# Linear attention and experts in one kernel: attention's short sums in named banks, leading rows' products later, the expert part's gathers in one written order

## The chip, the cores and the metric

The kernel runs on one core of a Trainium2 chip. Its engines are TensorE (PE in the rows, its weight loads PEld), VectorE (DVE), ScalarE (ACT), GpSimd (POOL) and SyncE (SP). The metric is the device time of one execution in microseconds (us); the kernel before has a median of 881.65 over three runs (881.14 to 881.79). All data is float32; a product of two float32 numbers is made from high and low parts in three passes.

## The reference

```
proj = x @ w_phi; proj -= max|proj|          # per row, 128 features
phi  = [exp(proj), exp(-proj)]               # 256 features, for q and k
kv   = phi(k).T @ v;  z = sum phi(k)         # per batch and head
x    = (phi(q) @ kv) / (phi(q) @ z + 1e-6)   # 8 batches x 8 heads x 576 rows x 64
x    = x as [4608 rows, 512]
logits = x @ w_gate;  e = argmax(logits);  gate = softmax(logits)[e]
out[row] = gate * (relu(x[row] @ w1[e]) @ w2[e])      # 8 experts, 512 -> 1024 -> 512
```

Each row of x goes to one of 8 experts; which one is known only at run time.

## The kernel before, in words

**Attention (0 to about 388 us).** 16 units of work, each two heads of two batches, in two halves (A and B, one per batch). In a half TensorE projects q and k (`ps_proj`), transposes exponentials (`pt`), adds up keys times values over the half (`pk`, the long sum, 30 matmuls), copies it out (`kvT`, by ACT at L410), multiplies it once more with small constants (`pf`, L419, copied to `kf` by VectorE at L430) and forms the outputs of the unit before (`pn`, L448). The order on TensorE is written by hand: `half` (L511) walks 30 slots and `chain` (L259) ties each matmul behind the one before; `book` (L506) puts other steps at a slot's number. One half is about 11.7 us long, a slot about 0.39.

**The pool of sums.** `pk` and the short sums `pf`, `prk` (counts that give each row its rank within its expert), `pc` and `pl` share a PSUM pool `ps_kv` of two buffers that are handed out in turn. `count_ranks` (L729) is booked at `RANK_AT` for three of the four groups of batches, the reduce and the three selects (L745 to L756, which read `prk`) at the slots behind it.

**The leading rows.** After three of four groups, the expert with most rows so far is picked (`pick_lead`, `find`), a 0/1 matrix `b` is built by VectorE (L838), and 54 products of three columns, `pl` (`find_rows`, L846, L849 and L850), give the numbers of its first 3 x 128 rows; `fetch` gathers them (POOL, L861), so that the expert part can begin with them.

**Expert part (from about 388 us).** Rows are sorted by expert into blocks of 128. A pair of blocks runs through `pair_first` (four times 24 matmuls of 256 columns into `pm`, L1123 to L1125), a relu by ACT (`hh`, L1130) and a remainder by VectorE (`hl`, L1131), and `pair_second` (four times 12 matmuls of 512 columns into `po`, L1143 to L1145); 19 pairs, then single blocks. A pair lasts about 22.5 us. `write` scales `po` with the row's gate into `ob` (ACT, L1191) and scatters it to the output (POOL, L1193). Each pair needs gathers on POOL: the rows `xg` (whole rows for the first pairs, from the fifth in eight quarter gathers, transposed by VectorE at L1099 into `px`), and the gates `gate`. In the code the gathers of pair u+2 and the gates of pair u+1 are called in the first quarter of pair u; where they stand on POOL the scheduler of the framework decides.

Of the kernel before, what the change touches and what calls it, by code (L numbers as in the profile page):

```python
# [9 lines left out]
F32 = mybir.dt.float32  # L10
# [46 lines left out]
def tile_linear_attention_moe(  # L57
# [36 lines left out]
    sg = late.enter_context(tc.tile_pool(name="sg", bufs=1, side="right"))  # L94
    ps_kv = late.enter_context(tc.tile_pool(name="ps_kv", bufs=2, space=PSUM, side="right"))
    hold = mid.enter_context(tc.tile_pool(name="hold", bufs=1, side="right"))
# [5 lines left out]
    ps_tr = early.enter_context(tc.tile_pool(name="ps_tr", bufs=2, space=PSUM, side="left"))  # L102


    w_bd = const.tile([P, 2 * F], F32, name="w_bd")
# [15 lines left out]
    for _ in range(WARM):  # L121
        pw = ps_kv.tile([P, 4, P], F32, name="pw", tag="pk")
        T.matmul(pw, ones, ones.unsqueeze(1).to_broadcast([P, 4, P]), start=True, stop=True)
# [75 lines left out]

    TOP_AT, RANK_AT, LEAD_AT = 78, 106, 166  # L200

# [48 lines left out]
    def behind(m, other):  # L250

        tc.add_manual_dep(
            m.ins,
            other.ins.name,
            mybir.DependencyInfo(mybir.DependencyClass.NoSync, mybir.DependencyReason.DATA),
            reason="order of the engine",
        )

    def chain(m):  # L259
# [109 lines left out]
    def kv_steps(st, bb):  # L369


        def step(hh, i, c, j):
            vh, vl = st["v"]
            if (hh, i, j) == (0, 0, 0):
                st["pk", bb] = ps_kv.tile([P, 2, 2 * F], F32, name="pk", tag="pk")
            n = D if j == 1 else D + 1
            kh, kl, s0 = st["kp", c]
            return T.matmul(  # L378
                st["pk", bb][0:n, hh, :],
                (vl if j == 1 else vh)[:, 2 * (c + (bb if c == 8 else 0)) + hh, 0:n],  # L380
                (kl if j == 2 else kh)[:, s0 + hh].rearrange("p s f -> p (s f)"),
                start=(hh, i, j) == (0, 0, 0),
                stop=(hh, i, j) == (1, 4, 2),
            )

        def whole(hh, i, c):
            if (hh, i) == (0, 0):
                st["pk", bb] = ps_kv.tile([P, 2, 2 * F], F32, name="pk", tag="pk")
# [264 lines left out]
    def route(g, lgc, c0, n, final=None):  # L653
# [55 lines left out]
        def count():  # L709
            if final:  # L710
                pc = ps_kv.tile([P, E], F32, name="pc", tag="pk")
                T.matmul(pc, ones, r["base"], start=True, stop=False)
# [92 lines left out]
    def lead():  # L805
# [4 lines left out]
        def pick_lead():  # L810
            pc = ps_kv.tile([P, E], F32, name="pc", tag="pk")
            T.matmul(pc, ones, bases[-1], start=True, stop=True)
# [33 lines left out]
        def find_rows():  # L846
            pl = ps_kv.tile([P, NLEAD], F32, name="pl", tag="pk")
# [12 lines left out]
    def fetch_rows(out, source, index, rows):  # L860
        return G.indirect_dma_start(  # L861
            out=out,
# [4 lines left out]
            oob_is_err=False,  # L867
        )

    def gather_rows(index, rows, after=None):  # L870
# [6 lines left out]
    def gather_quarters(b):  # L877


        xg = xgp.tile([P, 4, P], F32, name="xg")  # L880
        quarters = x_dram.rearrange("t (q d) -> (t q) d", q=4)
        for c in range(4):
            behind(fetch_rows(xg[:, c, :], quarters, qidx[:, c, b : b + 1], 4 * NT), st["experts"])
        return xg

    def gather_gates(b, after):
        gate = xgp.tile([P, XW], F32, name="gate", bufs=6)
        index, rows = (gidx0, NEARLY * P) if b < NLEAD else (gidx, NT)
        behind(fetch_rows(gate, g_dram, index[:, b : b + 1], rows), after)
        return gate  # L890
# [14 lines left out]
    for u, st in enumerate(units):  # L905
# [9 lines left out]
        if u % NPR == 0 and u > 0:  # L915
# [8 lines left out]
    kv_copy(prev, 1)  # L924
    slot[0] += 100
    take(len(queue))
# [45 lines left out]
    def tokens_of():  # L972

        pp = ps_kv.tile([P, NB], F32, name="pp", tag="pk")
        for j in range(NTILE):
# [9 lines left out]
    def quarters_of():  # L985
# [6 lines left out]
        )  # L992
        pq = ps_kv.tile([P, 4, NB], F32, name="pq", tag="pk")
        for c in range(4):
# [74 lines left out]

    def gather(u):  # L1070
        if u >= lim[0]:
            return
        for b in blocks(u):
            if ("xg", b) not in st:
                if b < NLEAD:
                    st["xg", b] = early_rows[b]
                elif by_quarters(u):
                    st["xg", b] = gather_quarters(b)
                else:
                    st["xg", b] = gather_rows(gidx[:, b : b + 1], NT, st.get("experts"))  # L1080

    def gates(u):
        if u < lim[0]:
            for b in blocks(u):
                if ("gate", b) not in st:
                    st["gate", b] = gather_gates(b, st["experts"])

# [25 lines left out]
    def pair_first(u, j, half=None):  # L1113
# [20 lines left out]
    def pair_second(u, j, half=None):  # L1134
        if j == 0:
# [10 lines left out]
        if j == 3 and half != 0:  # L1146
            for b, po in zip(blocks(u), st["po", u]):
                write(b, po)

    def first_product(u, n):  # L1150
# [37 lines left out]
    def write(b, po):  # L1188
# [3 lines left out]
        index = sidx0[:, b : b + 1] if b < NLEAD else sidx[:, b : b + 1]  # L1192
        G.indirect_dma_start(  # L1193
            out=out,
# [4 lines left out]
            oob_is_err=False,  # L1199
        )  # L1200

    r1 = route(NG - 1, lgc, 0, 6, False)
# [49 lines left out]
    quarters_of()  # L1252
    gates(1)
    gather(2)
# [13 lines left out]
    AHEAD_W = (((1, 2), (0, 7)), ((1, 3), (1, 4)), ((2, 0), (1, 5)), ((2, 1), (1, 6)))  # L1268
    for u in range(1, NPAIR):
        for j in range(4):  # L1270
            pair_first(u, j)
            if j > 1:
                x_parts(u + 1, j - 2)
            if (u, j) != (1, 0):
                pair_second(u - (j == 0), (j - 1) % 4)
            if j == 0:
                gather(u + 2)
                gates(u + 1)
            for du, k in AHEAD_W[j]:
                weights(u + du, k)  # L1280

    first_product(NPAIR, 0)
    pair_second(NPAIR - 1, 3)
# [107 lines left out]
```

## Time and profile before

| | before |
|---|---|
| median of 3 runs | 881.65 us (881.14 to 881.79) |
| the profiled execution | 882.15 us, of which the span 880.5 |
| TensorE busy | 865.2 us, 98% of the span |
| VectorE, ACT, POOL busy | 71%, 65%, 64% |
| mean granted clock | 0.991 of full |

The profile is of one execution. A row of the timeline gives the start and the length of one instruction (or of a run of equal ones, xN), its engine, its line, output <- inputs and, in brackets, how long the engine stood idle before it and what released it. The granted clock of TensorE has two levels, 1.0 and 0.5 of full speed; a number between is a mean over a stretch.

### The profile page before, as it was taken

To read this page: it belongs to the slowest core of one execution; us is meant where nothing else is said; L and a number is where in the kernel's file an instruction comes from. 1 tells how busy PE (TensorE), PEld (TensorE's weight loads), DVE (VectorE), ACT (ScalarE), POOL (GpSimd) and SP (SyncE) were. 2 spreads that over 40 slices of the span, in tenths; PEclk is the share of its full clock that TensorE was granted. 3 is DMA by queue.
4 is the path that set the end of the run, shared out by engine and by line. 5 is a ranking of instruction groups with operands and counts; after the bars stand their busy time and mean duration, and the time that the engine had idled before them with its cause. 6 is when DMAs were issued, how large, how long until landed. Compare 5 with 4: busy or idle time off the path is not lost. (4 is left out here: it accounts for less than half of the span.)

```text
span 880.5 us, 18049 instructions
## 1 busy us (share of the span) xinstructions
PE 865.2 (98%) x6605; PEld 811.7 (92%) x6605; DVE 623.7 (71%) x1044; ACT 572.6 (65%) x874; POOL 560.1 (64%) x407
## 2 busy tenths in 40 slices
PE   9999999999999999999899999999999999999997
PEld 6999999999999999999699999999999999999985
DVE  7678778887887788649487666666666666666451
ACT  6888888888888888653375555555555555555562
POOL 5667667776676677643666888867666666643342
PEclk9999999999999999899999999999999999999999
DMA  6233334333343333351344144541444653435650
GB/s 204 85 102 97 106 112 97 78 97 107 112 113 112 112 104 79 88 195 29 85 153 116 54 165 133 157 136 49 143 138 137 200 181 113 153 116 176 209 185 18
DMA packets 69692, 106.65 MB, mean 121 GB/s; under 512 B 13726, under 2 KB 31646, under 8 KB 69600
## 3 DMA queue, kind: packets, MB, share of 16 engines
q1 hardware_dynamic: 59312, 84.50, 31.9%
q0 software_dynamic: 9616, 20.81, 7.7%
q8 instruction: 53, 0.87, 0.4%
q14 instruction: 39, 0.32, 0.1%
q10 hardware_dynamic: 672, 0.15, 0.1%
HBM read 128.42 MB, written 20.26 MB: 169 GB/s over the span
## 5 line engine op out<-in xcount | busy, mean ns | idle before, releaser
L1058 DVE TENSOR_TENSOR wl<-raw,wh 128x1024 fp32r<-128x1024 f32 x160 | 196.8, 1235 | 108.0 <-ACT wh L1057 82.9
L1057 ACT CAST wh<-raw 128x1024 fp32r<-128x1024 f32 x168 | 174.9, 1047 | 84.6 <-PE po L1145 43.8
L861 POOL DMA_INDIRECT xg<-x_dram,qidx x132 | 163.9, 1242 | 84.2 <-DVE px L1099 39.5
L448 PE MATMUL pn<-kf,qp 128*128 128x73 f32 (+1 forms) x1152 | 185.5, 256 | 0.0
L313 POOL TENSOR_TENSOR kl<-e,kh 128x1024 fp32r<-128x1024 f32 x45 | 107.4, 2386 | 107.2 <-ACT kh L311 100.3
L1124 PE MATMUL pm<-xl,wh 128*128 128x256 f32 x608 | 173.3, 285 | 1.0 <-issue 0.9
L1125 PE MATMUL pm<-xh,wl 128*128 128x256 f32 x608 | 173.2, 285 | 0.3 <-issue 0.3
L1123 PE MATMUL pm<-xh,wh 128*128 128x256 f32 x608 | 172.4, 284 | 1.0 <-issue 1.0
L448 PEld LDWEIGHTS pn<-kf,qp 128*128 128x128 f32 x1152 | 172.6, 190 | 0.5
L285 DVE TENSOR_REDUCE mx<-ps_proj 128x4 f32<-128x512 f32 (+1 forms) x160 | 101.1, 632 | 59.7 <-PE ps_proj L281 58.0
L1124 PEld LDWEIGHTS pm<-xl,wh 128*128 128x128 f32 x608 | 117.2, 193 | 4.9 <-issue 2.0
L1143 PE MATMUL po<-wh,hh 128*128 128x512 f32 x304 | 120.1, 396 | 0.9 <-ACT hh L1130 0.9
L1123 PEld LDWEIGHTS pm<-xh,wh 128*128 128x128 f32 x608 | 117.1, 193 | 3.0 <-issue 0.2
L1144 PE MATMUL po<-wl,hh 128*128 128x512 f32 x304 | 119.5, 393 | 0.0
L1145 PE MATMUL po<-wh,hl 128*128 128x512 f32 x304 | 118.7, 391 | 0.0
L1125 PEld LDWEIGHTS pm<-xh,wl 128*128 128x128 f32 x608 | 117.3, 193 | 0.8 <-issue 0.7
L286 DVE TENSOR_TENSOR t<-ps_proj,mx 128x512 f32<-128x512 f32 (+1 forms) x160 | 101.4, 635 | 4.9
L378 PE MATMUL pk<-kh,vl 128*64 128x256 f32 x300 | 101.9, 340 | 0.0
L378 PE MATMUL pk<-kh,vh 128*65 128x256 f32 x300 | 99.9, 333 | 1.5 <-ACT kvT L410 1.5
L378 PE MATMUL pk<-kl,vh 128*65 128x256 f32 x300 | 100.4, 335 | 0.0
L245 POOL TENSOR_TENSOR xl<-xr,xh 128x640 fp32r<-128x640 f32 (+1 forms) x60 | 96.9, 1634 | 2.1 <-ACT xh L244 2.1
L1130 ACT ACTIVATE hh<-pm 128x512 fp32r<-128x512 f32 x76 | 45.4, 597 | 77.1 <-PE pm L1125 65.4
(217 smaller groups left out, 1905.2 us busy)
## 6 DMA issues: line engine op xcount, KB each, us to landing
raw<-w SPq DMA_DIRECT2D x168, 512.0 KB
vt<-vv SPq DMA_DIRECT2D x15, 640.0 KB
x_dram<-xrow SPq DMA_DIRECT2D x30, 256.0 KB
xr<-kT SPq DMA_DIRECT2D x15, 320.0 KB
xr<-qT SPq DMA_DIRECT2D x15, 320.0 KB
xr<-kT SPq DMA_DIRECT2D x17, 256.0 KB
xr<-qT SPq DMA_DIRECT2D x17, 256.0 KB
xg<-x_dram,qidx POOLq DMA_INDIRECT x132
```

Source lines behind the costliest of these rows:

```text
L313: eng.tensor_tensor(kl, e[:, 0:m], kh, op=ALU.subtract)
L378: return T.matmul(st["pk", bb][0:n, hh, :], (vl if j == 1 else vh)[:, 2 * (c + (bb if c == 8 else 0)) + hh, 0:n], (kl if j == 2 else kh)[: ...
L448: m = T.matmul(pn[:, i - a, :] if c < 8 else pn[:, 2 + hh : 6 : 2, :], qp[:, s, s0 + hh, :], st["kf"][:, hh, s, c // 4, :] if c < 8 else s ...
L861: return G.indirect_dma_start(out=out, out_offset=None, in_=source[0:rows], in_offset=bass.IndirectOffsetOnAxis(ap=index, axis=0), bounds_ ...
L1057: A.copy(th, raw[k])
L1058: m = (G if k in (POOL_LO0 if u == 0 else POOL_LO if u >= NPAIR else ()) else V).tensor_tensor(tl, raw[k], th, op=ALU.subtract)
L1123: T.matmul(pm[:, i], th, xh[:, k, :], start=(k == 0), stop=False)
L1124: T.matmul(pm[:, i], th, xl[:, k, :], start=False, stop=False)
L1125: T.matmul(pm[:, i], tl, xh[:, k, :], start=False, stop=(k == KD - 1))
L1143: T.matmul(po, hh[:, i, r], th[:, c], start=(i == j == 0), stop=False)
L1144: T.matmul(po, hh[:, i, r], tl[:, c], start=False, stop=False)
L1145: T.matmul(po, hl[:, i, r], th[:, c], start=False, stop=(i == 1 and j == 3))
```

## The change

1. `ps_kv` gets two named banks. The long sum `pk` changes the bank each half; a short sum that comes while long sums run takes the bank that the current long sum is not in. Outside attention the banks are taken in turn.
2. `RANK_AT` goes from 106 to 126: the ranks of three groups are counted 20 slots later, in the next half.
3. `find_rows` and `fetch` are booked 22 slots later than before (at 28 behind `LEAD_AT` instead of 6), and the 54 products of `pl` stand in TensorE's written order.
4. In the expert part, the gathers of pair u+2 are issued in four pieces of two quarters: after the first relu of pair u, between the two scatters of pair u-1, after the second relu, and after the third; the two gates of pair u itself after the fourth. The first, third and fourth piece and the gates wait for that relu; all POOL transfers of the loop stand in this one order (`lined`).

```diff
-    ps_kv = late.enter_context(tc.tile_pool(name="ps_kv", bufs=2, space=PSUM, side="right"))
+    ps_kv = late.enter_context(tc.tile_pool(name="ps_kv", bufs=1, space=PSUM, side="right"))
...
+    bank, summing = [0], [False]
+
+    def sums(shape, name, long=False):
+
+        if long or not summing[0]:
+            bank[0] ^= 1
+        summing[0] = long or summing[0]
+        b = bank[0] if long or not summing[0] else 1 - bank[0]
+        return ps_kv.tile(shape, F32, name=name, tag=f"pk{b}")
...
-    TOP_AT, RANK_AT, LEAD_AT = 78, 106, 166
+    TOP_AT, RANK_AT, LEAD_AT = 78, 126, 166
...
+    def paced(m, other):
+
+        if other is not None:
+            tc.add_manual_dep(
+                m.ins,
+                other.ins.name,
+                mybir.DependencyInfo(mybir.DependencyClass.Sync, mybir.DependencyReason.DATA),
+                reason="pace of the gathers",
+            )
+
+    behind_gather, lining = [None], [False]
+
+    def lined(m):
+
+        if behind_gather[0] is not None:
+            behind(m, behind_gather[0])
+        behind_gather[0] = m
...
-                st["pk", bb] = ps_kv.tile([P, 2, 2 * F], F32, name="pk", tag="pk")
+                st["pk", bb] = sums([P, 2, 2 * F], "pk", True)
...
-                st["pf"] = ps_kv.tile([P, 2, 2, W], F32, name="pf", tag="pk")
+                st["pf"] = sums([P, 2, 2, W], "pf")
...
-            r["prk"] = ps_kv.tile([P, 4 * P], F32, name="prk", tag="pk")
+            r["prk"] = sums([P, 4 * P], "prk")
...
-                T.matmul(pl, sel_p[:, j, :], r["b0"][:, j, :], start=(j == 0), stop=False)
-                T.matmul(pl, sel_h[:, j, :], r["b0"][:, j, :], start=False, stop=(j == NEARLY - 1))
+                chain(T.matmul(pl, sel_p[:, j, :], r["b0"][:, j, :], start=(j == 0), stop=False))
+                chain(T.matmul(pl, sel_h[:, j, :], r["b0"][:, j, :], start=False, stop=(j == NEARLY - 1)))
...
+    def gather_quarter(b, c, step):
+
+
+        if c == 0:
+            st["xg", b] = xgp.tile([P, 4, P], F32, name="xg")
         quarters = x_dram.rearrange("t (q d) -> (t q) d", q=4)
-        for c in range(4):
-            behind(fetch_rows(xg[:, c, :], quarters, qidx[:, c, b : b + 1], 4 * NT), st["experts"])
-        return xg
-
-    def gather_gates(b, after):
+        m = fetch_rows(st["xg", b][:, c, :], quarters, qidx[:, c, b : b + 1], 4 * NT)
+        behind(m, st["experts"])
+        paced(m, step)
...
-                book(60 * u + LEAD_AT, 3, lead())
+                pick, find, find_rows, fetch = lead()
+                book(60 * u + LEAD_AT, 3, [pick, find])
+                book(60 * u + LEAD_AT + 28, 3, [find_rows, fetch])
...
-        A.activation(hh, pm, AF.Relu)
+        st["step"] = A.activation(hh, pm, AF.Relu)
...
-            for b, po in zip(blocks(u), st["po", u]):
+            for i, (b, po) in enumerate(zip(blocks(u), st["po", u])):
                 write(b, po)
+                for f in between if i == 0 else ():
+                    f(None)
...
-    gates(1)
     gather(2)
...
     for u in range(1, NPAIR):
+        lining[0] = True
+        fetches, extra = gather_steps(u + 2), gate_steps(u)
+        n = len(fetches)
+        cuts = (0, 1, 1, 2, 2) if n == 2 else (0, 2, 4, min(n, 6), n)
+        parts = [fetches[a:b] for a, b in zip(cuts, cuts[1:])]
         for j in range(4):
             pair_first(u, j)
+            for f in (parts[0], parts[2], parts[3], ())[j]:
+                f(st["step"])
+            if j == 3:
+                for f in extra:
+                    f(st["step"])
             if j > 1:
                 x_parts(u + 1, j - 2)
             if (u, j) != (1, 0):
-                pair_second(u - (j == 0), (j - 1) % 4)
-            if j == 0:
-                gather(u + 2)
-                gates(u + 1)
+                pair_second(u - (j == 0), (j - 1) % 4, between=parts[1] if j == 0 else ())
```

On TensorE, at the leading rows' products in the last group of attention, before (`pt`, `pk`, `pn` are attention's own products, `pl` the leading rows'):

```order
L323 MATMUL pt<-ident,t 128x128
L378 MATMUL pk<-kl,vh_162 65x256
L448 MATMUL pn<-kf,qp 128x73
L849 LDWEIGHTS sel_p
L849 MATMUL pl<-b_5458,sel_p 128x3
L850 LDWEIGHTS sel_h
```

and after, 48 rows further on:

```order
L307 MATMUL ps_proj<-w_hi,xh 128x256
L308 MATMUL ps_proj<-w_lo,xh 128x256
L309 MATMUL ps_proj<-w_hi,xl 128x256
L476 MATMUL pn<-kf,qp 128x73
L877 LDWEIGHTS sel_p
L877 MATMUL pl<-b_5458,sel_p 128x3
```

The 48 rows between are attention's products that stood behind `pl` before.

On TensorE, at the third count of ranks (`prk`), before:

```order
L323 MATMUL pt<-ident,t 128x128
L378 MATMUL pk<-kh,vl_167 64x256
L448 MATMUL pn<-kf,qp 128x73
L732 LDWEIGHTS ltri
L732 MATMUL prk<-onehot,ltri 128x72
L735 LDWEIGHTS ones
```

and after:

```order
L447 MATMUL pf<-fold,kvT 128x73
L406 MATMUL pk<-kh,vh_162 65x256
L476 MATMUL pn<-kf,qp 128x73
L406 MATMUL pk<-kh,vl_164 64x256
L476 MATMUL pn<-kf,qp 128x73
L406 MATMUL pk<-kl,vh_162 65x256
L476 MATMUL pn<-kf,qp 128x73
L406 MATMUL pk<-kh,vh_162 65x256
L351 MATMUL pt<-ident,t 128x128
L406 MATMUL pk<-kh,vl_164 64x256
L351 MATMUL pt<-ident,t 128x128
L760 LDWEIGHTS ltri
```

The weight load of `ltri` begins the count. It moved from the middle of one half to behind the four `pf` of the next; `pk` here is the long sum that runs meanwhile in the other bank.

On POOL in the steady expert loop, one pair, before (`out<-ob` is a scatter, `xg` a quarter gather, `gate` the gather of a block's gates):

```order
L1193 DMA out<-ob,sidx 4608x512
L861 DMA gate<-g_dram,gidx 128x4 x2
L861 DMA xg<-x_dram,qidx 128x128 x2
L1193 DMA out<-ob,sidx 4608x512
L861 DMA xg<-x_dram,qidx 128x128 x6
L1193 DMA out<-ob,sidx 4608x512
L861 DMA gate<-g_dram,gidx 128x4 x2
```

and after:

```order
L889 DMA gate<-g_dram,gidx 128x4 x2
L889 DMA xg<-x_dram,qidx 128x128 x2
L1248 DMA out<-ob,sidx 4608x512
L889 DMA xg<-x_dram,qidx 128x128 x2
L1248 DMA out<-ob,sidx 4608x512
L889 DMA xg<-x_dram,qidx 128x128 x4
L889 DMA gate<-g_dram,gidx 128x4 x2
```

The gates moved from behind the first scatter to behind the last quarter gathers, and belong to the pair at work, no longer to the next; two gathers stand between the scatters, as before, and two ahead of them.

## Rows read from the trace of the kernel before

**Rows 1.** The page's first part: busy time, share of the span, instructions
```profile
PE 865.2 (98%) x6605; PEld 811.7 (92%) x6605; DVE 623.7 (71%) x1044; ACT 572.6 (65%) x874; POOL 560.1 (64%) x407
```

**Rows 2.** Stretches of 20 us: length, busy us of each engine, granted clock, DMA
```profile
360.00:380.00 20.00, 18.16 (x190) 18.03 (x189) 11.36 (x29) 8.35 (x17) 8.94 (x6) 0.83 0.49 151
420.00:440.00 20.00, 16.33 (x94) 13.46 (x94) 7.74 (x14) 7.82 (x11) 13.26 (x13) 0.94 0.33 94
440.00:460.00 20.00, 20.00 (x119) 18.36 (x119) 16.19 (x17) 14.38 (x18) 12.96 (x9) 0.89 0.45 132
640.00:660.00 20.00, 20.00 (x132) 18.31 (x131) 13.76 (x15) 11.34 (x15) 12.68 (x11) 1.00 0.45 130
```

**Rows 3.** What TensorE waited for: engine, line, releaser, us in total, times, longest
```profile
PE pl L849 <- DVE b L838: 1.8, 1, 1.8
PE pk L378 <- ACT kvT L410: 1.5, 3, 0.5
PE pm L1123 <- issue: 1.0, 2, 0.6
PE pm L1124 <- issue: 0.9, 1, 0.9
```

**Rows 4.** TensorE over time at the leading rows' products: start, us, instruction, idle before
```profile
363.69 0.34 PE L448 MATMUL pn<-kf,qp 128*128 128x73 f32 x2
365.87 0.17 PE L849 MATMUL pl<-b,sel_p 128*128 128x3 bf16 x1 [1.84 <-DVE b L838]
```

**Rows 5.** VectorE over time, the work that those products wait for
```profile
365.56 0.25 DVE L838 TENSOR_TENSOR b<-iota_p,bl 128x81 bf16<-128x81 f32 x1
```

**Rows 6.** Stretches of 2 us, columns as in group 2
```profile
362.00:364.00 2.00, 2.00 (x19) 1.90 (x19) 2.00 (x7) 0.11 (x1) 1.27 (x1) 1.00 0.00 0
366.00:368.00 2.00, 2.00 (x58) 2.00 (x56) 0.23 (x2) 1.59 (x3) 0.06 (x1) 0.50 0.62 211
416.00:418.00 2.00, 2.00 (x70) 1.81 (x68) 1.47 (x3) 0.00 (x0) 0.00 (x0) 1.00 0.04 8
436.00:438.00 2.00, 0.81 (x3) 0.63 (x4) 0.00 (x0) 0.00 (x0) 1.70 (x2) 0.91 0.08 2
```

**Rows 7.** VectorE and TensorE over time round a count of ranks
```profile
335.11 0.23 DVE L740 TENSOR_TENSOR rks<-prk,onehot 128x72 f32<-128x72 f32 x1 [0.28 <-PE prk L738]
340.22 0.33 PE L378 MATMUL pk<-kh,vh 128*65 128x256 f32 x1 [0.50 <-ACT kvT L410]
341.76 0.54 DVE L756 TENSOR_TENSOR sel<-iota_p,prk 128x384 bf16<-128x384 f32 x1
344.05 0.34 PE L419 MATMUL pf<-fold,kvT 65*128 65x73 f32 x2
344.86 0.45 DVE L430 COPY kf<-pf 128x292 f32<-128x292 f32 x1
```

**Rows 8.** POOL and ACT over time in one pair of the expert loop
```profile
644.84 1.62 POOL L861 DMA_INDIRECT gate<-g_dram,gidx  x1 [0.30 <-issue]
653.50 0.59 ACT L1130 ACTIVATE hh<-pm 128x512 fp32r<-128x512 f32 x1
659.07 0.60 ACT L1130 ACTIVATE hh<-pm 128x512 fp32r<-128x512 f32 x1 [1.88 <-PE pm L1125]
661.08 1.42 ACT L1191 ACTIVATE ob<-po,gate 128x512 f32<-128x512 f32 x2 [1.41 <-PE po L1145]
664.74 0.59 ACT L1130 ACTIVATE hh<-pm 128x512 fp32r<-128x512 f32 x1
```

**Rows 9.** POOL's row gathers and the TensorE instructions that read what they fetch
```profile
367.94 1.28 POOL L861 DMA_INDIRECT xg<-x_dram,gidx  x1 [4.66 <-DVE sidx L852]
387.78 0.64 PE L1104 MATMUL px<-ident,xg 128*128 128x128 f32 x4
418.79 1.03 POOL L861 DMA_INDIRECT xg<-x_dram,gidx  x1 [5.98 <-DVE emp L980]
422.28 0.75 PE L1104 MATMUL px<-ident,xg 128*128 128x128 f32 x4 [0.48 <-DMA xg<-x_dram,gidx]
```

More of the change, by code (lines that the diff above doesn't have):

```diff
@@ L121, in tile_linear_attention_moe @@
     for _ in range(WARM):
-        pw = ps_kv.tile([P, 4, P], F32, name="pw", tag="pk")
+        pw = sums([P, 4, P], "pw")
         T.matmul(pw, ones, ones.unsqueeze(1).to_broadcast([P, 4, P]), start=True, stop=True)
@@ L387, in whole @@
             if (hh, i) == (0, 0):
-                st["pk", bb] = ps_kv.tile([P, 2, 2 * F], F32, name="pk", tag="pk")
+                st["pk", bb] = sums([P, 2, 2 * F], "pk", True)
             e, _, s0 = st["kp", c]
@@ L710, in count @@
             if final:
-                pc = ps_kv.tile([P, E], F32, name="pc", tag="pk")
+                pc = sums([P, E], "pc")
                 T.matmul(pc, ones, r["base"], start=True, stop=False)
@@ L810, in pick_lead @@
         def pick_lead():
-            pc = ps_kv.tile([P, E], F32, name="pc", tag="pk")
+            pc = sums([P, E], "pc")
             T.matmul(pc, ones, bases[-1], start=True, stop=True)
@@ L846, in find_rows @@
         def find_rows():
-            pl = ps_kv.tile([P, NLEAD], F32, name="pl", tag="pk")
+            pl = sums([P, NLEAD], "pl")
             for j in range(NEARLY):
-                T.matmul(pl, sel_p[:, j, :], r["b0"][:, j, :], start=(j == 0), stop=False)
-                T.matmul(pl, sel_h[:, j, :], r["b0"][:, j, :], start=False, stop=(j == NEARLY - 1))
+                chain(T.matmul(pl, sel_p[:, j, :], r["b0"][:, j, :], start=(j == 0), stop=False))
+                chain(T.matmul(pl, sel_h[:, j, :], r["b0"][:, j, :], start=False, stop=(j == NEARLY - 1)))
             V.tensor_scalar(gidx0, pl, -1.0, 0.0, op0=ALU.add, op1=ALU.max)
@@ L860, in fetch_rows @@
     def fetch_rows(out, source, index, rows):
-        return G.indirect_dma_start(
+        m = G.indirect_dma_start(
             out=out,
@@ L868, in fetch_rows, with gather_rows @@
         )
-    def gather_rows(index, rows, after=None):
+        if lining[0]:
+            lined(m)
+        return m
+    def gather_rows(index, rows, after=None, step=None):
         xg = xgp.tile([P, 4, P], F32, name="xg")
@@ L874, in gather_rows, with gather_gates @@
             behind(m, after)
+        paced(m, step)
         return xg
-    def gather_quarters(b):
-        xg = xgp.tile([P, 4, P], F32, name="xg")
+    def gather_quarter(b, c, step):
+        if c == 0:
+            st["xg", b] = xgp.tile([P, 4, P], F32, name="xg")
         quarters = x_dram.rearrange("t (q d) -> (t q) d", q=4)
-        for c in range(4):
-            behind(fetch_rows(xg[:, c, :], quarters, qidx[:, c, b : b + 1], 4 * NT), st["experts"])
-        return xg
-    def gather_gates(b, after):
+        m = fetch_rows(st["xg", b][:, c, :], quarters, qidx[:, c, b : b + 1], 4 * NT)
+        behind(m, st["experts"])
+        paced(m, step)
+    def gather_gates(b, after, step=None):
         gate = xgp.tile([P, XW], F32, name="gate", bufs=6)
         index, rows = (gidx0, NEARLY * P) if b < NLEAD else (gidx, NT)
-        behind(fetch_rows(gate, g_dram, index[:, b : b + 1], rows), after)
+        m = fetch_rows(gate, g_dram, index[:, b : b + 1], rows)
+        behind(m, after)
+        paced(m, step)
         return gate
@@ L924, in tile_linear_attention_moe @@
     kv_copy(prev, 1)
+    summing[0] = False
     slot[0] += 100
@@ L972, in tokens_of @@
     def tokens_of():
-        pp = ps_kv.tile([P, NB], F32, name="pp", tag="pk")
+        pp = sums([P, NB], "pp")
         for j in range(NTILE):
@@ L992, in quarters_of @@
         )
-        pq = ps_kv.tile([P, 4, NB], F32, name="pq", tag="pk")
+        pq = sums([P, 4, NB], "pq")
         for c in range(4):
@@ L1068, in by_quarters, with rows_of, gates_of, gather_steps @@
         return u >= 4
-    def gather(u):
+    def rows_of(b, u, step):
+        st["xg", b] = gather_rows(gidx[:, b : b + 1], NT, st.get("experts"), step)
+    def gates_of(b, step):
+        st["gate", b] = gather_gates(b, st["experts"], step)
+    def gather_steps(u):
         if u >= lim[0]:
-            return
+            return []
+        steps = []
         for b in blocks(u):
@@ L1077, in gather, with gate_steps @@
                 elif by_quarters(u):
-                    st["xg", b] = gather_quarters(b)
+                    steps += [lambda step, b=b, c=c: gather_quarter(b, c, step) for c in range(4)]
                 else:
-                    st["xg", b] = gather_rows(gidx[:, b : b + 1], NT, st.get("experts"))
+                    steps += [lambda step, b=b: rows_of(b, u, step)]
+        return steps
+    def gate_steps(u):
+        if u >= lim[0]:
+            return []
+        return [lambda step, b=b: gates_of(b, step) for b in blocks(u) if ("gate", b) not in st]
+    def gather(u):
+        for f in gather_steps(u):
+            f(None)
     def gates(u):
[L1083 to L1086, printed above, removed]
+        for f in gate_steps(u):
+            f(None)
     def x_parts(u, i):
@@ L1129, in pair_first, with pair_second @@
         hl = mp.tile([P, 2, 2 * P], F32R, name="hl", bufs=4)
-        A.activation(hh, pm, AF.Relu)
+        st["step"] = A.activation(hh, pm, AF.Relu)
         V.scalar_tensor_tensor(hl, pm, 0.0, hh, op0=ALU.max, op1=ALU.subtract)
         st["hp", u, j] = (hh, hl)
-    def pair_second(u, j, half=None):
+    def pair_second(u, j, half=None, between=()):
         if j == 0:
@@ L1146, in pair_second @@
         if j == 3 and half != 0:
-            for b, po in zip(blocks(u), st["po", u]):
+            for i, (b, po) in enumerate(zip(blocks(u), st["po", u])):
                 write(b, po)
+                for f in between if i == 0 else ():
+                    f(None)
     def first_product(u, n):
@@ L1192, in write @@
         index = sidx0[:, b : b + 1] if b < NLEAD else sidx[:, b : b + 1]
-        G.indirect_dma_start(
+        m = G.indirect_dma_start(
             out=out,
@@ L1200, in write @@
         )
+        if lining[0]:
+            lined(m)
     r1 = route(NG - 1, lgc, 0, 6, False)
@@ L1274, in tile_linear_attention_moe @@
             if (u, j) != (1, 0):
-                pair_second(u - (j == 0), (j - 1) % 4)
-            if j == 0:
-                gather(u + 2)
-                gates(u + 1)
+                pair_second(u - (j == 0), (j - 1) % 4, between=parts[1] if j == 0 else ())
             for du, k in AHEAD_W[j]:
                 weights(u + du, k)
+    lining[0] = False
     first_product(NPAIR, 0)
```

## The prediction

> **What bounds the kernel now.** I read the busy times first: TensorE is busy 98% of the span and no other engine above 71% [rows 1]. So a gain must be a place where TensorE stands still or runs at the lower clock. Then the stretches of 20 us, to find such places [rows 2]: in the steady expert loop (640 to 660 is like every stretch from 460 to 860) TensorE is busy 20.00 of 20.00 at clock 1.00, so nothing that only reorders POOL can make that part shorter. The exceptions beside start and end are 360 to 380 (18.16 busy, clock 0.83), 420 to 440 (16.33, 0.94) and 440 to 460 (busy throughout, 0.89). Third, what TensorE waited for [rows 3]: one wait of 1.8 for `b` ahead of the leading rows' products, three of 0.5 for `kvT`, and gaps of 1.0 and 0.9 in front of the first expert products that no releaser explains. Then the timeline at each.
>
> The leading rows' products start at 365.87 after 1.84 of standing still; the last matmul before them started at 363.69 [rows 4]. VectorE finishes `b`, which they need, at 365.56 + 0.25 = 365.81 [rows 5]. Right behind that wait the granted clock is at 0.50, the lower of its two levels (1.2 GHz) [rows 6]. The 0.83 over 360 to 380 says for how long: 20 x 0.17 / 0.5 = 6.8 us at half clock [rows 2]. TensorE is busy throughout it, so it lost half, 3.4.
>
> **The change part by part.** The sum is made against the profiled execution (882.15: a span of 880.5 and 1.65 outside it), which is 0.5 above the median of the three runs (881.65). All terms lie in the span, so I subtract the same from the median.
>
> *Leading rows' products later.* find_rows and fetch are booked 22 slots later, which in TensorE's order is 48 matmuls. At full clock 19 matmuls are recorded in 2.00 us [rows 6], so they come due at about 363.9 + 48 x 2 / 19 = 369.0. `b` is ready at 365.8, 3.2 ahead, and its VectorE work keeps its place in the order. The wait goes: -1.84, bounded by 0 and -1.84. If the clock fell because TensorE stood still, the low stretch goes with it: another -3.4. Its ends are 0 (it only moves) and -3.4. I take -3.4: the clock is at 1.00 up to the wait and at 0.50 directly behind it. The one other candidate is the burst of 54 three-column products itself (58 matmuls in 366 to 368). A longer burst of much the same kind, the token lists' products (44 columns each), fills 416 to 418, 70 matmuls in 2 us; the clock stays 1.00 there [rows 6].
> The Trainium skill, page "TensorE: Matmul & The Clock Gate", section "Why this matters for your kernels", says that only an idle gap longer than this one sends the clock down; by that, the wait is not the cause and the 3.4 would stay. The row above differs from it, as the fall comes right behind the shorter gap. By the page the sum would be 3.4 smaller; that is the second rival below.
> What is late next: the first early row gather starts 2.1 after the first product (367.94 against 365.87) and its reader needs it at 387.78, without waiting [rows 4, 9]. Now it starts at about 371.1, behind one more POOL split of keys perhaps 2.4 later still (an estimate from POOL's 1.27 of work in 362 to 364 [rows 6], doubled). The reader comes 5.2 earlier, at 382.5. A row gather has been seen to land within 3.5 of its start (418.79 to 422.28 [rows 9]); three in a row from 373.5 at 1.6 each land by about 380.3. Hidden, by some 2 us.
>
> *Sums in named banks, ranks counted later.* Before, the count of ranks takes one of the two buffers in turn, so that the next long sum `pk` gets the buffer of the last one and waits 0.50 for its copy `kvT` (340.22 is one of three [rows 3, 7]). With the long sums alternating and the short ones always in the bank beside, the new long sum's bank was read out a half ago. -1.5 for the three, bounded by 0. Two new sharings could give it back. First, the ranks now follow the folded sums `pf` in one bank and need their copy `kf` done: it ends at 345.31, some 1.2 after the last pair of `pf` started at 344.05 [rows 7]; the ranks stand 11 matmuls behind that, 11 x 2 / 19 = 1.2. This is a tie: up to 0.3 each, 0.9 in all. Second, the bank must be free for the long sum that starts 52 matmuls after the ranks, 5.5 us. It is held until the last of three selects; from `rks` to there VectorE has 0.23, three small steps (0.2 each), one projection's maximum and subtraction (0.7 each, an estimate from 2.00 busy for 7 instructions in 362 to 364 [rows 6]), 3 x 0.54: some 4 us. (Before it was 335.11 to 342.30, with much else between [rows 7].) Hidden by 1.5.
>
> *Expert part: one written order on POOL.* Per pair the same 12 POOL DMAs: eight quarter gathers, two scatters, two gates. No instruction is added on TensorE, ACT or VectorE, and their order in the steady loop stays but for VectorE's transposes of the gathered rows, which stand one `hl` later (a quarter of a pair, while their readers come most of a pair later). POOL is busy 12.68 of 20 [rows 2], so the order fits. Term: 0, since TensorE has no idle time to give. The one thing that becomes late is the gates: they were fetched a pair ahead; now they wait for the pair's own last relu (`hh` ends at 654.09) and the gate copies `ob` want them at 661.08 [rows 8]. POOL has nothing else by then; with 0.30 + 1.62 for each [rows 8], the second starts at 656.3 and, by the 3.5 above, has landed by 659.8. Early enough by 1.3; and TensorE is held only if `ob` (to 662.50) runs past the relu at 664.74, another 2.2 later [rows 8]. What queues behind a late gate on POOL is the next pair's gathers, a pair ahead of use.
>
> *Routing and the end.* The last count of ranks stands 19 rows later, behind work that VectorE must do anyway: 0, within 0.3. At the end two transposes now stand before a `hl` of the last full pair and wait for gathers that come late in POOL's new order: 0, at worst one gather's 1.6 [rows 8].
>
> *The first pairs.* Between 434 and 439 TensorE has its unexplained gaps (0.81 busy in 436 to 438 [rows 6]), and behind them half clock: 20 x 0.06 / 0.5 + 20 x 0.11 / 0.5 = 6.8 us, 3.4 lost [rows 2]. Together with the gaps of 1.0 and 0.9 [rows 3]: 5.3. POOL fetches three gates in a row just there, and the change takes these away. But the gaps have no releaser in the profile, and pairs of gates elsewhere bring none. Bounds -5.3 and +2 (the gaps move and meet a longer burst); I take 0, like the rest of the loop where POOL is as full.
>
> Sum: -1.84 - 3.4 - 1.5 = -6.7. From the median: 874.9; I say 875.0. Its own range is 873.5 to 877.5: it takes in the ties at the ranks (0.9) and at the end (1.6).
>
> **The rivals.**
> 1. *The gaps at 434 to 439 go too.* For it: POOL's burst of gates is dissolved just there. Against: no releaser, and full POOL queues elsewhere are harmless. 875.0 - 5.3 = 869.7.
> 2. *The clock falls all the same*, a little later, with the narrow products. For it: they are the only such burst inside attention; and the page named above. Against: the token lists at 416. 875.0 + 3.4 = 878.4.
> 3. *Slower: gates come too late.* Each of 18 pairs then holds `ob`, and TensorE with it. From the rows the second gate must land more than 3.5 + 1.3 + 2.2 = 7 us after its issue before TensorE pays; from there each microsecond costs 18. At one microsecond beyond, 875.0 + 18 = 893; the gain is eaten at 0.37. For it: POOL's strict order puts every paced DMA behind its wait. Against: the margin.
> 4. *Nothing*: the ranks or the products find a new wait in the bank that they now share, and the low clock stays: 875.0 + 3.4 + 1.5 + 0.9 = 880.8 or a little more.
>
> **How the numbers follow.** Forecast 0.43, rival 1 0.24, rival 2 0.12, rival 4 0.09, rival 3 0.12. A difference of 0.2% (1.8 us) is what a measurement of this kernel can tell from no change, so faster means below 879.9: the forecast and rivals 1 and 2, 0.79. Rival 4 is the same, 0.09; rival 3 slower, 0.12. The range leaves out rival 3 and a little at either end: 868.0 to 881.0.
>
> **What would show it.** In the profile after: no wait of `pl` for `b`, and clock 1.00 for the whole stretch where 0.83 stood; no wait of `pk` for `kvT`, nor a new one of `prk` for `kf` or of `pk` for `sel`; the loop at 20.00 of 20.00; `ob` released by TensorE's `po`, not by the gates' DMA. A stretch at half clock behind the narrow products speaks for rival 2, a clean stretch behind the first pairs for rival 1, `ob` released by a DMA for rival 3. Wrong would be a gain outside these places, or a loop with idle time on TensorE.

## The result, and the profile after

| | before | after |
|---|---|---|
| median | 881.14 us (9 runs) | 873.01 us (9 runs, 871.52 to 874.20) |
| ratio to before | | 0.9905, 95% interval 0.9888 to 0.9921 |
| span of the profiled execution | 880.5 us | 871.7 us |

The kernel is 0.95% faster, 8.1 us by the medians and 8.8 by the two profiled spans. 875.0 was forecast, with a range of 868.0 to 881.0. Where an interval below is wide, single executions of one kernel differed by some us (one of the nine runs of before took 873.94), probably because the stall of the first pairs that is told of here isn't alike in each.

The waits of TensorE after (engine, line, releaser, us in total, times, longest), against [rows 3]:

```profile
PE po L1198 <- DVE hl L1184: 2.6, 1, 2.6
```

The rest of its list is three waits in the first 14 us (2.5 in all) and one of 0.2. The waits of `pl` for `b`, of `pk` for `kvT` and the unexplained gaps ahead of `pm` are gone. A wait of 2.6 for `hl` is new. The stretches of 20 us (length, busy us of PE, PEld, DVE, ACT and POOL, granted clock, DMA share, GB/s), against [rows 2]:

```profile
360.00:380.00 20.00, 20.00 (x235) 20.00 (x233) 13.18 (x37) 10.51 (x20) 10.98 (x7) 1.00 0.54 173
420.00:440.00 20.00, 20.00 (x136) 18.51 (x136) 18.70 (x19) 15.58 (x20) 6.59 (x5) 1.00 0.37 126
440.00:460.00 20.00, 20.00 (x136) 18.52 (x135) 10.89 (x12) 10.19 (x14) 10.93 (x10) 1.00 0.58 186
640.00:660.00 20.00, 20.00 (x126) 17.96 (x125) 15.00 (x16) 11.17 (x16) 12.42 (x12) 1.00 0.41 129
820.00:840.00 20.00, 17.39 (x72) 13.92 (x71) 13.80 (x14) 11.96 (x17) 14.68 (x11) 0.91 0.61 186
```

Where 18.16 at clock 0.83 and 16.33 at 0.94 stood, TensorE is busy throughout at clock 1.00; the steady loop is as it was; and 820 to 840, which was full, has 17.39 at 0.91.

The leading rows' products, against [rows 4, 5]: TensorE's timeline (start, length, instruction) and VectorE's:

```profile
369.04 0.17 PE L877 MATMUL pl<-b,sel_p 128*128 128x3 bf16 x1
```

```profile
365.26 0.24 DVE L866 TENSOR_TENSOR b<-iota_p,bl 128x81 bf16<-128x81 f32 x1
```

`b` is ready at 365.50, the products start at 369.04, with no bracket: nothing was waited for.

In the loop, against [rows 8]: POOL's second gate, and ACT:

```profile
642.35 0.99 POOL L889 DMA_INDIRECT gate<-g_dram,gidx  x1 [0.31 <-issue]
```

```profile
647.63 1.42 ACT L1246 ACTIVATE ob<-po,gate 128x512 f32<-128x512 f32 x2 [1.44 <-PE po L1198]
```

The second gate is issued at 642.35, right behind the pair's fourth relu. `ob` at 647.63 is released by TensorE's `po`, not by the gates.

And the place that lost: VectorE, two of POOL's last three row gathers for the single blocks, TensorE, and two stretches, after:

```profile
820.22 2.12 DVE L1152 STREAM_TRANSPOSE px<-xg 128x512 f32<-128x512 f32 x2 [8.32 <-DMA xg<-x_dram,qidx]
822.23 0.69 DVE L1184 SCALAR_TENSOR_TENSOR hl<-pm,hh 128x512 fp32r<-128x512 f32 x1
```

```profile
813.11 1.02 POOL L889 DMA_INDIRECT xg<-x_dram,qidx  x1 [0.31 <-issue]
815.74 0.99 POOL L889 DMA_INDIRECT xg<-x_dram,qidx  x1 [0.30 <-issue]
```

```profile
822.97 0.67 PE L1198 MATMUL po<-wh,hl 128*128 128x512 f32 x1 [2.60 <-DVE hl L1184]
```

```profile
812.00:820.00 8.00, 8.00 (x57) 7.44 (x56) 0.00 (x0) 3.05 (x4) 4.04 (x5) 1.00 0.89 314
824.00:826.00 2.00, 2.00 (x7) 1.51 (x6) 2.00 (x4) 0.00 (x0) 1.69 (x2) 0.50 0.04 5
```

VectorE stands still for 8.32 until row gathers of the single blocks have landed, transposes, and only then makes the `hl` that TensorE has waited for since 820.37. The last three gathers were issued at 813.11, 814.43 and 815.74; the trace's semaphore records put their landings at 819.81, 819.88 and 820.54 (for the last two a few records are missing), 4.8 to 6.7 later. In the meantime the DMA engines are 89% busy, most of it with weights. Behind the wait the clock is at 0.50.

Summed over the program, by the start of the last product into `po` of each pair (us of the profiled executions; the other columns are the experiments below):

| stretch | before | after | products later | banks | both of these | gathers | singles earlier |
|---|---|---|---|---|---|---|---|
| start to the end of pair 0 | 424.0 | 418.1 | 419.4 | 422.8 | 418.3 | 424.0 | 418.4 |
| pair 1 | 34.0 | 26.4 | 30.1 | 34.6 | 34.3 | 26.6 | 26.4 |
| pairs 2 to 17 | 360.7 | 360.9 | 360.6 | 360.6 | 362.0 | 361.7 | 361.2 |
| pair 18 | 22.3 | 26.8 | 22.3 | 22.3 | 22.3 | 26.6 | 22.3 |
| the rest | 39.5 | 39.5 | 39.5 | 39.5 | 39.4 | 39.5 | 39.5 |

Attention gave 5.9, pair 1 gave 7.6, pair 18 took 4.5 back. The first row contains that executions don't start alike: the second copy `kvT` stands at 31.5 before and at 32.0 after. Counted from that copy, the stretch is shorter by 6.4 after, by 4.6 with the products later, by 1.5 with the banks and by 6.2 with both.

### The profile page after: what moved, and what is told of

Read it like the earlier page. It is cut to its first block, busy times and chain, and to the rows that moved or that the text cites. A ratio compares the mean times of both kernels' runs of the same rounds, so it can differ in the third digit from the quotient of the medians.

```text
span 871.7 us, 18059 instructions
## 1 busy us (share of the span) xinstructions
PE 859.9 (99%) x6605; PEld 807.1 (93%) x6605; DVE 623.0 (71%) x1044; ACT 571.3 (66%) x874; POOL 547.1 (63%) x407
## 5 line engine op out<-in xcount | busy, mean ns | idle before, releaser
L889 POOL DMA_INDIRECT xg<-x_dram,qidx x132 | 152.1, 1152 | 83.6 <-ACT hh L1183 49.0
L1152 DVE STREAM_TRANSPOSE px<-xg 128x512 f32<-128x512 f32 x33 | 37.0, 1124 | 93.6 <-DMA xg<-x_dram,qidx 91.3
```

The costliest lines, as they stand in the source:

```text
L889: m = G.indirect_dma_start(out=out, out_offset=None, in_=source[0:rows], in_offset=bass.IndirectOffsetOnAxis(ap=index, axis=0), bounds_che ...
```

## Experiments

**Products later, alone.**

```diff
+                chain(T.matmul(pl, sel_p[:, j, :], r["b0"][:, j, :], start=(j == 0), stop=False))
...
-                book(60 * u + LEAD_AT, 3, lead())
+                pick, find, find_rows, fetch = lead()
+                book(60 * u + LEAD_AT, 3, [pick, find])
+                book(60 * u + LEAD_AT + 28, 3, [find_rows, fetch])
```

> The kernel before with only find_rows and fetch booked 22 slots later and their products in the written order. Theory (the clock fell because TensorE stood still): the wait of 1.84 for b and the low-clock stretch go, clock 1.00 in 360 to 380, the gaps of the first pairs stay with their own low clock: 881.1 - 5.2 = 875.9. Rival (the narrow products bring the clock down wherever they stand): a stretch at 0.50 behind them remains, 879.3.

877.16 (5 runs), ratio 0.9942, interval 0.9885 to 0.9999. The stretch of 20 us and the first product:

```profile
360.00:380.00 20.00, 20.00 (x234) 20.00 (x233) 12.74 (x34) 10.09 (x20) 12.11 (x8) 1.00 0.52 166
```

```profile
370.05 0.17 PE L849 MATMUL pl<-b,sel_p 128*128 128x3 bf16 x1
```

The products start at 370.05 without a wait and the clock stays at 1.00 with the same burst of narrow products in the stretch. So the low clock followed the standing still, as forecast, and not the products by themselves. All twelve traces agree: the clock falls behind the wait for `b` in the four that have it, and stays at 1.00 there in the eight that don't. This kernel's profiled execution has smaller gaps in pair 1 than before (30.1 against 34.0), so its span says more than this edit; the attention part alone is 4.6 shorter.

**Banks and later ranks, alone.**

```diff
-    TOP_AT, RANK_AT, LEAD_AT = 78, 106, 166
+    TOP_AT, RANK_AT, LEAD_AT = 78, 126, 166
...
+                st["pk", bb] = sums([P, 2, 2 * F], "pk", True)
...
+                st["pf"] = sums([P, 2, 2, W], "pf")
...
```

> The kernel before with only the named banks and RANK_AT 126. Theory: the three waits of pk for kvT go, 881.1 - 1.5 = 879.6, and nothing else. Rival (prk waits for kf, or pk for the selects): new waits of some 0.3 each, 880.5 or more.

883.15 (10 runs), ratio 1.0011 (0.9988 to 1.0033): no gain. Neither theory. The waits:

```profile
PE po L1154 <- issue: 3.7, 1, 3.7
PE pl L859 <- DVE b L848: 2.6, 1, 2.6
PE pk L388 <- DVE sidx L862: 0.4, 1, 0.4
```

The three waits for `kvT` are gone, but the leading rows' products, still early, wait 2.6 for `b` instead of 1.8, and the next long sum waits 0.4 until they leave the bank that they now share. The waits alone come out even (1.3 gone, 0.7 and 0.4 new). Attention ends 1.2 earlier in this execution, since the stretch at half clock behind the wait is 3.4 long and not 6.8; pair 1 loses 0.6 of it.

**Both of these, without the order of gathers.**

```diff
+    TOP_AT, RANK_AT, LEAD_AT = 78, 126, 166
...
+                book(60 * u + LEAD_AT + 28, 3, [find_rows, fetch])
...
```

> The kernel before with named banks, RANK_AT 126 and the leading rows' products later, without the new order of gathers. Theory (the banks alone gained nothing because the products, still early, then waited longer for b and held the bank against the next long sum; with the products late both waits are gone): no wait of pl or pk, clock 1.00 in 360 to 380, gaps of the first pairs as in the kernel before: 881.5 - 6.7 = 874.8. Rival (the shared bank costs something by itself): 877 or more, with a wait of pk or pl left.

876.65 (4 runs), ratio 0.9951 (0.9932 to 0.9970). No wait of `pl` or `pk`; what is left at the top of its list is in pair 1, and the clock stays at 1.00 behind it:

```profile
PE pm L1137 <- DVE hl L1144: 2.4, 1, 2.4
PE po L1156 <- issue: 2.2, 1, 2.2
```

```profile
420.00:440.00 20.00, 15.92 (x103) 13.88 (x102) 10.39 (x10) 10.57 (x14) 13.18 (x11) 1.00 0.29 84
440.00:460.00 20.00, 17.65 (x114) 15.89 (x114) 14.59 (x17) 11.80 (x16) 12.74 (x10) 1.00 0.59 171
```

Attention ends 5.7 earlier, as much as in the kernel after (5.9). The stall of pair 1 stays (34.3). The theory holds, its number was 1.9 too low: 5.7 and not 6.7, and 1.3 more in pairs 2 to 17. These 1.3 lie in one pair, at 738 to 740, where TensorE has gaps without a releaser of 0.33 and 0.22 at the end of a run of POOL's transfers.

**The order of gathers, alone.**

```diff
-        return ps_kv.tile(shape, F32, name=name, tag=f"pk{b}")
+        return ps_kv.tile(shape, F32, name=name, tag="pk")
...
-    TOP_AT, RANK_AT, LEAD_AT = 78, 126, 166
+    TOP_AT, RANK_AT, LEAD_AT = 78, 106, 166
...
-                book(60 * u + LEAD_AT + 28, 3, [find_rows, fetch])
+                book(60 * u + LEAD_AT, 3, lead())
```

> The kernel after with the old bookings and one tag for the sums, so only the expert part's order of gathers, gates and scatters is changed. Theory (the gaps of the first pairs come from POOL's order there, the wait for hl near the end too): gaps and low clock at 434 to 445 gone (-7), a wait of po for hl with low clock near 825 (+4.4): 878.5. Rival (the gaps went because attention ends earlier, not by POOL's order): gaps stay and the tail costs 4.4: 885.5.

879.46 (10 runs), ratio 0.9956 (0.9934 to 0.9978).

```profile
PE po L1196 <- DVE hl L1182: 3.0, 2, 2.4
PE pl L877 <- DVE b L866: 1.9, 1, 1.9
PE pk L406 <- ACT kvT L438: 1.5, 3, 0.5
```

The old waits in attention are back, the gaps of pair 1 are not (26.6), and pair 18 has its wait for `hl`. So POOL's order makes both the gain in pair 1 and the loss in pair 18.

**Singles earlier: the loss in pair 18 undone, on the kernel after.**

```diff
-        fetches, extra = gather_steps(u + 2), gate_steps(u)
+        fetches, extra = gather_steps(u + 2 + (u == NPAIR - 1)), gate_steps(u)
+        if u == NPAIR - 2:
+            fetches += gather_steps(u + 3)
```

> The kernel after with one edit: the row gathers of the first two single blocks are issued in the last pair but one, those of the third in the last pair, so that four gathers and not eight stand on POOL ahead of the transposes that precede hl. Theory (the wait of 2.6 for hl and the low clock behind it, 1.8 lost, come from those transposes waiting for late gathers): both go, 873.0 - 4.4 = 868.6. Rival (hl is late for VectorE's weight splits, or another wait takes its place): 872 to 873.

869.45 (4 runs), ratio to before 0.987 (0.982 to 0.992): the fastest of all. The stretch that had 17.39 at 0.91:

```profile
820.00:840.00 20.00, 20.00 (x96) 16.65 (x95) 12.44 (x12) 14.48 (x20) 10.10 (x8) 1.00 0.57 173
```

Pair 18 is back at 22.3. The theory holds; the gain is 3.6 by medians that were measured apart, 3.9 by the spans.

**Gates of pairs 2 and 3 held back, on the kernel before.**

```diff
-                gates(u + 1)
+                if u > 2:
+                    gates(u + 1)
+            if j == 2 and u <= 2:
+                gates(u + 1, st["step"])
...
```

With `st["step"]` the gates wait for that relu.

> The kernel before with one edit: the gates of pairs 2 and 3 wait for a relu of the pair ahead, so that POOL no longer fetches three gates in a row while the first pair ends; the rest of the loop keeps the scheduler's order. Theory (that burst of gates makes the gaps): no gaps at 434 to 439, no low clock behind, 881.1 - 6.8 = 874.3. Rival (the gaps come from something else in that place): gaps stay, 881.

903.81 (4 runs), ratio 1.021 (1.0131 to 1.0289): a miss for both. In pair 1 no gap without a releaser is left; it takes 31.1, with a wait of 2.5 for `hh` and half clock behind it. But the edit put 32 transfers in one run on POOL (465 to 512), and there such gaps are more and longer. Three neighbouring products of the second kind, which stand 0.23 apart otherwise, start 0.73 and 0.70 apart (504.89, 505.62 and 506.32). It doesn't tell whether the gates made the gaps of before, since all of the order behind them moved too.

**A run of gates in the steady loop, on the kernel after.**

```diff
+                if u == 8:
+                    more_gates(12)
...
```

> The kernel after with twelve more gate gathers (of one block, into a spare tile, read by nobody) in one run on POOL behind the gates of the ninth pair, in the middle of the steady loop. Theory (a run of back-to-back gate gathers on POOL holds up TensorE's sequencer): gaps without a releaser of 1 to 3 us in the stretch of that run, some 590 to 610, with low clock behind: 875 to 880. Rival (such a run is harmless by itself; the gaps of the first pairs need something else that is there): no gap, 873.

888.82 (8 runs), ratio 1.0079 (1.0053 to 1.0105). Slower, but not by the theory:

```profile
PE po L1204 <- DVE wl L1096: 9.0, 1, 9.0
PE pm L1184 <- issue: 0.2, 1, 0.2
```

```profile
623.52 1.09 DVE L1158 STREAM_TRANSPOSE px<-xg 128x512 f32<-128x512 f32 x1 [12.97 <-DMA xg<-x_dram,qidx]
```

Only 0.2 of gaps without a releaser. The 12 gathers delay the row gathers behind them by some 15 (the first starts at 615.64, where a pair's 22.5 behind the last one's 578.49 is 601.0); VectorE waits 12.97 for these in front of a transpose, and the product waits 9.0 for what VectorE has behind it. It is the wait of pair 18 once more, dosed. The run of gates by itself held up nothing in this execution: TensorE has no gap while its fourteen transfers stand in a row (595 to 615).

**The written order without the waits for the relus, on the kernel after.** The manual dependency of `paced` is left out.

```diff
-        if other is not None:
+        if False:
             tc.add_manual_dep(
...
```

> The kernel after without the waits for the relus; the written order of gathers, gates and scatters stays. Theory 1 (the gaps of the first pairs went because gates no longer follow one another three in a row): no gaps, 873 within 1. Theory 2 (they went because the waits break POOL's unbroken runs of transfers): gaps without a releaser and low clock come back in the first pairs, 877 to 880.

893.77 (4 runs), ratio 1.0152 (1.0098 to 1.0206). Outside both expectations. One pair of many, VectorE and TensorE:

```profile
509.18 1.11 DVE L1152 STREAM_TRANSPOSE px<-xg 128x512 f32<-128x512 f32 x1 [5.30 <-DMA xg<-x_dram,qidx]
510.21 0.66 DVE L1184 SCALAR_TENSOR_TENSOR hl<-pm,hh 128x512 fp32r<-128x512 f32 x1
```

```profile
510.92 0.50 PE L1198 MATMUL po<-wh,hl 128*128 128x512 f32 x1 [0.74 <-DVE hl L1184]
```

Without the waits the scheduler puts both transposes of a pair ahead of the same `hl`, where one `hl` stood between them in the kernel after (why it does so isn't shown). VectorE waits 5.30 for a gather, and TensorE for `hl`, pair after pair (pairs 2 to 17 take 384.0 and not 360.9). The waits for the relus are thus worth 20 us, most of it by the place they give to the transposes. The profile also lists some 6 us of gaps without a releaser. 3.6 of them are two gaps ahead of the product that reads `hl`, right behind the end of `hl`, so they are the same wait. Of the 2.6 that are left, 0.7 is in the first pairs, and most of the rest in the steady loop, at the end of a run of 12 transfers (734 to 750):

```profile
748.12 0.37 PE L1176 MATMUL pm<-xh,wh 128*128 128x256 f32 x1 [0.81 <-issue]
749.54 0.28 PE L1178 MATMUL pm<-xh,wl 128*128 128x256 f32 x1 [0.93 <-issue]
```

They start 1.42 apart. That is for theory 2, but small beside the rest.

**The same, in the first three pairs only.**

```diff
-                f(st["step"])
+                f(st["step"] if u > 3 else None)
...
-                    f(st["step"])
+                    f(st["step"] if u > 3 else None)
```

> The kernel after with the waits for the relus left out in the first three pairs only; the written order stays everywhere. Theory 2 (unbroken runs of POOL's transfers, as the first pairs then have, hold up the other engines' sequencers): gaps without a releaser between 415 and 450 and low clock behind them, 875 to 880. Theory 1 (the order of gates and scatters alone removed the gaps): none, 873 within 1.

877.42 (5 runs), ratio to before 0.9953 (0.9927 to 0.9979): in the range of theory 2 by the time, but not by the gaps.

```profile
PE po L1198 <- DVE hl L1184: 4.7, 3, 2.9
PE po L1196 <- issue: 0.7, 1, 0.7
```

Pair 1 takes 28.7: 2.3 more than after, 5.3 less than before, with one gap of 0.7 without a releaser and no low clock in the first pairs. So the order alone takes away most of the stall, the waits the rest. POOL has seven transfers back to back here (417 to 426), where before had eleven (423 to 438).

**And with five gates more there.**

```diff
+            if (u, j) == (1, 1):
+                more_gates(5)
...
```

> The kernel after without the waits for the relus in the first three pairs (as in the run before) and with five more gate gathers (into a spare tile, read by nobody) on POOL where the first pair ends, so that POOL has about twelve transfers back to back there, as the kernel before had. Theory 2 (a long unbroken run of POOL's transfers at this place holds up the other engines' sequencers): gaps without a releaser of 2 to 4 us between 424 and 440, in steps of about 0.7, pair 1 some 5 longer than in the run without them (28.7): 881 or more. Rival (the run of transfers is harmless here too, as in the steady loop): gaps as without the five, 877.5.

882.48 is the median of eight runs, but they lie in two groups, four from 875.75 to 877.48 and four from 887.48 to 891.95. The profiled execution took 887.48. POOL, first and last of its twelve; TensorE in the same stretch; and the stretch of 20 us:

```profile
418.48 1.04 POOL L889 DMA_INDIRECT xg<-x_dram,gidx  x1 [0.16 <-issue]
...
433.31 0.99 POOL L889 DMA_INDIRECT gate<-g_dram,gidx  x1 [0.30 <-issue]
```

```profile
431.20 0.28 PE L1182 MATMUL pm<-xh,wh 128*128 128x256 f32 x1 [0.92 <-issue]
432.67 0.28 PE L1182 MATMUL pm<-xh,wh 128*128 128x256 f32 x1 [0.95 <-issue]
434.09 0.37 PE L1184 MATMUL pm<-xh,wl 128*128 128x256 f32 x1 [1.01 <-issue]
434.82 0.37 PE L1183 MATMUL pm<-xl,wh 128*128 128x256 f32 x1
435.53 0.58 PE L1184 MATMUL pm<-xh,wl 128*128 128x256 f32 x1 [0.34 <-issue]
```

```profile
420.00:440.00 20.00, 15.97 (x90) 13.79 (x89) 8.04 (x8) 9.03 (x12) 12.10 (x12) 0.84 0.29 81
```

Pair 1 takes 35.8, 7.1 more than without the five. TensorE's products, otherwise 0.12 apart, come in steps: 1.47, 1.42, 0.73, 0.71 (431.20, 432.67, 434.09, 434.82, 435.53). Some of SyncE's register steps at the same time take 0.70 each (at 430.47, 431.92 and 434.78). One gap of 0.67, at 426.07, is there without the five too (0.7); the others start about ten transfers into POOL's run, and the clock falls to a mean of 0.84. Now the same place in the kernel before, POOL's first and last transfer of its run of eleven, and TensorE:

```profile
423.44 1.03 POOL L861 DMA_INDIRECT gate<-g_dram,gidx  x1 [0.31 <-issue]
...
437.17 1.00 POOL L861 DMA_INDIRECT gate<-g_dram,gidx  x1 [0.30 <-issue]
```

```profile
435.55 0.28 PE L1123 MATMUL pm<-xh,wh 128*128 128x256 f32 x1 [0.33 <-issue]
436.27 0.38 PE L1125 MATMUL pm<-xh,wl 128*128 128x256 f32 x1 [0.33 <-issue]
437.69 0.57 PE L1124 MATMUL pm<-xl,wh 128*128 128x256 f32 x1 [0.93 <-issue]
439.11 0.37 PE L1123 MATMUL pm<-xh,wh 128*128 128x256 f32 x1 [0.63 <-issue]
```

The steps are the same (0.72, 1.42, 1.42), late in POOL's run, and in both traces they stop within 1.3 of its end. So lengthening POOL's run at this place made the stall of before anew, in the execution that was profiled. By their times four of the eight executions don't have it, and none of the five without the added gates has it (the longest took 879.64). That speaks for the length of the run as one condition; it isn't enough by itself.

## Why the prediction was right, and where it wasn't

- *Products later, -1.84.* Right, to the place: 369.0 said, 369.04 found, `b` ready 3.5 ahead (3.2 said), the first early gather at 371.04 (371.1 said) and its reader at 382.16 (382.5 said) without a wait.
- *The low stretch, -3.4.* The mechanism held: the clock fell behind the wait for `b` in each of the four traces that have it (1.84 to 2.58 long), and products later alone keeps it at 1.00. So rival 2 did not happen. The Trainium skill ("TensorE: Matmul & The Clock Gate", "Why this matters for your kernels") has only a longer idle gap bring the clock down. This case's traces differ from it: the clock fell behind 1.84 here, in the run of gathers alone behind 1.86, and in pair 18 behind 2.60. But a gap of this length doesn't always do it: with both attention edits the clock stayed at 1.00 behind gaps of 2.18 and 2.35 in pair 1. The narrow products don't do it without a gap; whether they help behind one, no run separates. The term was mis-sized. Attention ends 4.6 earlier with this edit, not 5.2. I took it that half the time at half clock is lost; the same kind of product, in the kernel before, at half and at full clock:

```profile
368.52 0.42 PE L279 MATMUL ps_proj<-w_hi,xh 128*128 128x256 f32 x1
368.74 0.41 PE L280 MATMUL ps_proj<-w_lo,xh 128*128 128x256 f32 x1
368.95 0.41 PE L281 MATMUL ps_proj<-w_hi,xl 128*128 128x256 f32 x1
...
375.17 0.28 PE L279 MATMUL ps_proj<-w_hi,xh 128*128 128x256 f32 x1
375.28 0.28 PE L280 MATMUL ps_proj<-w_lo,xh 128*128 128x256 f32 x1
```

They stand 0.21 to 0.22 apart at the low clock and 0.11 to 0.12 at the full one: a factor of 1.8. Of 6.8 that is a loss of 3.0, and 1.84 + 3.0 = 4.8. The stretch itself isn't the same in each execution: of the four traces with the wait, two have 6.8 at half clock and two 3.4.
- *Named banks, -1.5.* With the products late, the step from 4.6 to 5.7 in the table: -1.1. The three waits themselves went from 0.50 to 0.08 of idle time each (19.92 busy in a stretch of 20 where 19.50 stood), 1.3 in all. The two ties that I feared brought no wait. What I had not seen is that this part alone gains nothing: the products, left early, share a bank with the long sum. Together the attention part gave 5.9, or 6.4 from an equal start, where 6.7 was forecast.
- *The loop, 0.* Right: 360.7 and 360.9. The gates come in time, with more to spare than I gave them (the second is issued 5.3 ahead of its reader, 4.8 said); rival 3 did not happen. What no rival had is the cost of late row gathers, with VectorE's transposes waiting for them and `hl` behind these: the run of gates in the steady loop lost 16 us by it, and the order without the waits most of its 21.
- *The end, "0, at worst one gather's 1.6".* This step failed. It cost 4.5: a wait of 2.6 for `hl`, and 3.4 at half clock behind it. I named the place, but the 1.6 is POOL's own time for issuing one transfer. What counted was the landing, up to 6.7 after the issue with the DMA engines 89% busy; even the 3.5 of [rows 9], from a stretch in which they were 22% busy, would have been too low. And I priced no clock behind the wait.
- *The first pairs, "I take 0".* This step failed too: -7.6, rival 1, which I had priced at 5.3 (the idle time for `hh` and the smaller gaps went as well). I gave it 0.24. "The rest of the loop where POOL is as full" was the wrong argument: the run of before in 467 to 590 is longer and has no gap, so a full POOL isn't enough, yet at this place its order decides.

The two failed steps cancel in part (-7.6 and +4.5), and the attention part gave somewhat less than its 6.7. That 875.0 came out 2 us from 873.01 is luck to this extent: by the signs that the prediction had named, what happened is its attention part and rival 1 together, and a loss at the end that no rival had.

Open: why POOL's run holds up TensorE and SyncE, and only in some places and executions. Runs of 12 to 76 transfers in the steady loop of before have no gap; runs of other kernels have some (one of 32 with the gates held back, one of 12 in the order without the waits). The last experiment speaks for the run's length at the place of the first pairs, not for what else is needed. One candidate stands in the traces and no run tests it: where the gaps are, nearly each transfer takes 1.0 on POOL and the next follows 0.3 later; in the run of 76 half take 1.4 to 2.0, and in that with the twelve added gates three of fourteen take 1.4 to 1.7.

## What to carry to other kernels

Read a wait on TensorE together with the clock behind it: in the profiled execution of before the clock's part (3.0) was larger than the wait (1.84). It is worth less than half of the slow time, since products slow by 1.8 and not by 2, and one execution doesn't say how long the slow stretch is in the others. When gathers are tied to a pace, look at every in-order engine that reads them: an early transpose that waits for a late gather costs whatever stands behind it, and a bound on landing must come from a stretch with as busy a DMA. An edit that frees one buffer may gain nothing until the neighbour that shares it is moved too.

## What the runs showed of the hardware that was not expected

- Late in some of POOL's runs of back-to-back indirect transfers, TensorE starts products in steps of 0.70 to 0.73 us, or about twice that, and SyncE has steps of 0.70; no releaser is shown.
- The clock fell behind gaps of 1.84, 1.86 and 2.60 us, and stayed at 1.00 behind gaps of 2.18 and 2.35 in another trace and behind three of 0.50. Products of 256 columns at the low clock are 1.8 times as far apart as at the full one.
- Quarter gathers landed 4.8 to 6.7 us after their issue with the DMA engines 89% busy.
